# Eight idle matmuls placed at four products, in the PSUM bank each product is about to write

## The chip, the core and the metric

The kernel runs on one core of one Trainium2 chip. The metric is the device time of one execution in microseconds (us). Its five engines are named as in the profile: PE is TensorE (matrix products; PEld is its weight load), DVE is VectorE, ACT is ScalarE, POOL is GpSimd and SP is SyncE, which here only issues transfers (DMAs). PE writes to PSUM, which has eight banks; DVE and ACT read it from there.

## The reference

Two blocks are computed one after the other, in float32, for 4 batches, 4 heads of 32, 1088 tokens and a model width of 128:

```python
def phi(x):                                    # r = 8
    a = np.einsum('rd,bhsd->bhsr', S1, x)
    b = np.einsum('rd,bhsd->bhsr', S2, x)
    return np.einsum('bhsi,bhsj->bhsij', a, b).reshape(*x.shape[:-1], r * r)
q_p, k_p = (phi(q), phi(k))
kv = np.einsum('bhsf,bhsd->bhfd', k_p, v)
z = np.sum(k_p, axis=2)
num = np.einsum('bhsf,bhfd->bhsd', q_p, kv)
den = np.einsum('bhsf,bhf->bhs', q_p, z)[..., None] + 1e-06
x = num / den                                  # then (B, S, H*D)
...
theta = x @ w_theta
zr, zi = x * np.cos(theta), x * np.sin(theta)
y = np.einsum('ts,bsd->btd', w_tok_r, zr) + np.einsum('ts,bsd->btd', w_tok_i, zi)
u = x + y
out = u + np.maximum(u @ w_ch, 0.0)
```

The products with the two 1088x1088 token matrices are most of the arithmetic.

## The kernel before

Every piece of work is registered as an operation ("op") with a number in the order of registration: an engine, the buffers it writes and reads, and a function that issues its instructions. The order in which the ops are issued is not that of registration. It is written out in the string ORDER, a list of the 1015 numbers 0 to 1014, and the string PLACES gives each buffer its slot. A PSUM buffer's slot (class "ps", 0 to 7) is one of the eight banks. Each engine runs its own ops strictly in the order of ORDER. Between engines an op waits for what it reads, and a buffer that takes over a slot waits until every reader of the buffer that had the slot is done: the pool of PSUM tiles has one tile per slot.

A filler is one matmul that computes nothing that is used: `spin` multiplies a zeroed 128x384 bfloat16 tile `idle` with 128 of its own columns. It writes to the PSUM buffer `nowhere`, which sits in bank 3. Ten of them form op 1, at the start. One more is op 126, a normal op of the order; it is the last use of `nowhere`, and behind it bank 3 goes to another buffer. The string SPINS adds fillers ahead of chosen ops, as pairs "op:count"; `Layout.issue` issues them just before the op's own instructions, on PE.

Batches 0 and 1 go first. For each batch a chain of tiny operations turns the Gram matrix of the keys into the key sums' small matrices. It has three products on PE, with DVE and ACT work between them. For batch 1 (function `chain`, with stage name "chain1") these are:

| op | what it is | writes to bank | waits for | the bank's buffer before, and its last reader |
|---|---|---|---|---|
| 166 | first product (`first`) | `tp`, 5 | op 164 (DVE, e1) and op 165 (ACT, e0) | Gram matrix `kk`, read last by op 164 |
| 172 | second product (`second`) | `np`, 4 | op 170 (DVE) and op 171 (ACT), both `tac` | key features of batch 3, read by op 228 (ACT) |
| 174 | sum over partitions with `ones` | `pt`, 1 | op 173 (DVE, m4) | key features of batch 1 (`kf`), read last by op 143 (DVE) |

Around them the order of PE is: op 126 (filler), 189 and 197 (transposes and features of keys), 166, 191, 227, 209, 203 (key features, and a small sum), 132 and 138 (products of key features and values, batch 1), 172, 439 and 441 (transposes of the query features of batch 0), 174, 144 (the last third of the products begun by 132 and 138), 443 (numerator of batch 0). The order of DVE there is: 163, 433, 164, 318, 434, 167 (reads `tp`), 435, 168, 436, 169, 437, 170, 438 (query features), 143 (outer products of batch 1's key features, read from PSUM bank 1), 173 (reads `np`), 452, 175 (reads `pt`). ACT copies the key features with ops 228, 204, 192 in this order, and later the transposed query features with 442 and 440.

Op 422 is the first of three products that form the levels of batch 0's queries (`levels`, function `lev`). It reads the small matrices `mv` and `mf` of batch 0, which the last DVE steps of batch 0's chain (ops 117 to 122) write.

Batches 2 and 3 share their token products in a Winograd form, and the last of these products is issued in pieces. Op 1010 is the very last transpose on PE (`turn` in `finish_turned`, one matmul instruction with the identity for 128 columns; `times` beside it multiplies the same columns by `w_ch`). It writes to bank 7 (`ut`), waits for op 999 (DVE, which adds the last piece of the product to `xT`), and follows op 1005 (transpose) and op 1006 (product with `w_ch`) of the piece before. The buffer that had bank 7 before was last read by op 979 (DVE).

## Time and profile before

| | |
|---|---|
| three runs | 222.03, 223.25 and 223.28 us (median 223.25) |
| the profiled execution | 221.87 us in all; its span, first to last instruction, 220.1 us |
| PE | busy 211.9 us, 96% of the span, 2045 matmul instructions |
| DVE | busy 173.8 us, 79% |
| ACT | busy 116.8 us, 53% |
| fillers in the trace (line 350) | 20: ten at 1.34 us, two at 4.92, four at 7.80, one each at 15.81, 19.29, 25.26 and 32.59 |

All times in views are in us from the start of the span. In the timeline a row merges neighbouring instructions of a kind: start, length from the first start to the last end, engine, line, what is written and read, and how many instructions. A matmul's row lasts longer than its share of the pipeline, since matmuls overlap: what counts for throughput is the distance from one start to the next. An arithmetic product of float32 operands is two matmul instructions. Most helpers share a line: L312 is any product through `mm`, L292 any DVE `tensor_tensor`, L694 and L1010 are transposes of keys and of query features, L710 is the ACT copy of key features, L1014 that of query features.

### The profile page before, as it was taken

How to read it: one execution, taken by the hardware profiler on the slowest of the kernel's cores; microseconds unless marked ns; L12 is line 12 of the kernel's file. 1: busy time of each engine (PE TensorE's matmuls, PEld its weight loads, DVE VectorE, ACT ScalarE, POOL GpSimd, SP SyncE). 2: the span in 40 equal slices, each digit the busy share in tenths (PEclk: the TensorE clock that was granted, in tenths of full speed). 3: DMA queues.
4: the chain of work that ended last, by engine and by line, in shares of the span. 5: the costliest groups of instructions: out<-in, count | busy, mean ns of one | idle time of the engine just before them, and what ended most of it. 6: DMA issues, size and time to landing. Idle time of an engine off the chain costs nothing.

```text
span 220.1 us, 5075 instructions
## 1 busy us (share of the span) xinstructions
PE 211.9 (96%) x2045; PEld 160.0 (73%) x2045; DVE 173.8 (79%) x395; ACT 116.8 (53%) x228; POOL 22.7 (10%) x44
## 2 busy tenths in 40 slices
PE   7999996999999999999999999999999999999993
PEld 3787895776678576766667668777688888788872
DVE  4799999999989998988906852899268899955651
ACT  3899989779978986646424455623484000000000
POOL 2465000000050110000222040000200000000000
PEclk9999999999999999999999999999999999999999
DMA  5999189993969763785345342003400002102453
GB/s 177 421 416 390 35 368 356 337 414 102 357 207 255 211 251 133 283 324 206 79 139 91 119 107 42 1 13 56 66 0 0 3 0 47 25 0 43 66 91 75
DMA packets 23195, 34.68 MB, mean 158 GB/s; under 512 B 17028, under 2 KB 18308, under 8 KB 20996
## 3 DMA queue, kind: packets, MB, share of 16 engines
q1 hardware_dynamic: 17908, 29.28, 37.8%
q0 software_dynamic: 1728, 4.65, 9.9%
q10 hardware_dynamic: 3536, 0.43, 1.3%
q8 instruction: 16, 0.26, 0.5%
q14 instruction: 7, 0.06, 0.1%
HBM read 27.48 MB, written 2.23 MB: 135 GB/s over the span
## 4 chain that ended last, share of the span: by engine, by line
PE 83%; DVE 11%; ACT 2%; issue 2%; POOL 1%; POOLq 0%
PE ps L312 74%; PE ps L1010 3%; DVE big L292 3%; DVE g L292 2%; PE ps L1043 2%; PE ps L350 2%; DVE lv L292 1%; PE ps L918 1%; DVE sm L299 1%; DVE hf L296 1%; DVE sm L292 1%; PE ps L694 1%; ACT big L605 1%; ACT g L697 1%; DVE big L296 0%
## 5 line engine op out<-in xcount | busy, mean ns | idle before, releaser
L312 PE MATMUL ps<-big,zs 128*128 128x384 f32 (+4 forms) x398 | 111.6, 423 | 0.4 <-DVE big L292 0.4
L312 PEld LDWEIGHTS ps<-big,zs 128*128 128x128 f32 x398 | 71.2, 190 | 26.7 <-issue 0.8
L1142 ACT COPY g<-ps 128x128 f32<-128x128 f32 (+1 forms) x3 | 0.9, 301 | 48.1 <-PE ps L1134 44.6
L557 ACT ACTIVATE big<-zs 128x1088 int32<-128x1088 uint32 (+1 forms) x18 | 21.1, 1178 | 6.4 <-DMA zs<-w_tok 4.7
L292 DVE CUSTOM_DVE_ANT_0 big<-big,big 128x2176 uint16<-128x2176 uint16 x17 | 21.7, 1284 | 1.5 <-ACT big L557 1.5
L312 PE MATMUL ps<-big,big 128*64 128x64 f32 (+2 forms) x208 | 21.6, 276 | 0.0
L555 ACT ACTIVATE big<-zs 128x1088 f32<-128x1088 f32 x17 | 20.6, 1216 | 0.2 <-DMA zs<-w_tok 0.2
L312 PEld LDWEIGHTS ps<-big,big 128*64 128x64 f32 (+1 forms) x208 | 16.7, 154 | 3.0 <-issue 0.5
L292 DVE TENSOR_TENSOR big<-big,big 128x544 f32<-128x544 f32 x24 | 16.7, 714 | 0.1
L1014 ACT COPY g<-ps 128x384 f32<-128x384 f32 x24 | 10.3, 485 | 11.1 <-PE ps L1010 10.1
L292 DVE TENSOR_TENSOR zs<-ps,g 128x768 f32<-128x768 f32 (+2 forms) x20 | 12.5, 629 | 3.0 <-ACT g L1056 2.6
L306 POOL DMA_DIRECT2D big<-hf x6 | 5.9, 985 | 82.6 <-DVE sm L296 40.7
L296 DVE TENSOR_SCALAR big<-big 128x1088 int32<-128x1088 int32 x17 | 12.1, 718 | 0.1
L292 DVE TENSOR_TENSOR g<-lv 128x768 f32<-128x768 f32 x12 | 11.0, 953 | 0.6 <-PE ps L312 0.5
L312 PEld LDWEIGHTS ps<-w,big 128*128 128x128 f32 x80 | 10.3, 192 | 1.6 <-issue 0.6
L299 DVE SCALAR_TENSOR_TENSOR g<-g,ps 128x384 f32<-128x384 f32 x12 | 6.5, 549 | 5.9 <-ACT g L1052 5.7
L312 PE MATMUL ps<-w,big 128*128 128x128 f32 x80 | 11.1, 277 | 0.0
L1052 ACT ACTIVATE g<-ps 128x384 f32<-128x384 f32 x12 | 5.7, 490 | 7.9 <-PE ps L312 5.3
L1010 PEld LDWEIGHTS ps<-ident,g 128*128 128x128 f32 x72 | 8.2, 141 | 2.3 <-issue 0.8
L1010 PE MATMUL ps<-ident,g 128*128 128x128 f32 x72 | 9.5, 275 | 0.0
L299 DVE SCALAR_TENSOR_TENSOR big<-ps,even,big 128x256 f32<-128x256 f32 (+1 forms) x10 | 4.8, 495 | 5.7 <-PE ps L312 5.7
L312 PE MATMUL ps<-g,sm 128*64 128x384 f32 x48 | 9.1, 499 | 0.0
(185 smaller groups left out, 335.6 us busy)
## 6 DMA issues: line engine op xcount, KB each, us to landing
zs<-w_tok SPq DMA_DIRECT2D x17, 1088.0 KB, 7.0
big<-k_l SPq DMA_DIRECT2D x6, 576.0 KB, 5.9
big<-hf POOLq DMA_DIRECT2D x6, 576.0 KB, 5.6
big<-q_l SPq DMA_DIRECT2D x4, 576.0 KB, 8.7
big<-v_l SPq DMA_DIRECT2D x4, 576.0 KB, 11.0
g<-big POOLq DMA_DIRECT2D x4, 192.0 KB, 3.7
out<-g SPq DMA_DIRECT2D x16, 48.0 KB, 1.8
g<-big POOLq DMA_DIRECT2D x2, 160.0 KB, 3.2
```

The lines of the kernel that those rows point to most:

```text
L292: eng.tensor_tensor(out=o, in0=a, in1=b, op=f)
L296: (eng or V).tensor_scalar(out=o, in0=a, scalar1=s1, scalar2=s2, op0=op0, **kw)
L299: (eng or V).scalar_tensor_tensor(out=o, in0=a, scalar=s, in1=b, op0=op0, op1=op1)
L306: op("G", 0.9, lambda: G.dma_start(dst(), src(), accum_op=ALU.add), w, r, fly=fly)
L312: T.matmul(o, lhs, rhs, start=start, stop=stop, skip_group_check=True)
L350: T.matmul(nowhere(), idle()[:, 0:P], idle(), start=True, stop=True, skip_group_check=True)
L555: op("A", 0.22 + n * 0.0009, lambda: A.activation(dfn(), words_of(raw(), n)[1].bitcast(F32), AF.Prelu, scale=2.0**-112, alpha=-(2.0**32)), ...
L557: op("A", 0.22 + n * 0.0009, lambda: A.activation(stp(), words_of(raw(), n)[0].bitcast(U32), AF.Copy, scale=2.0**-29), [stp], [raw])
L1010: T.transpose(tr()[:, i * P:(i + 1) * P], qp()[:, i * H + 2 * n:i * H + 2 * n + 2].rearrange("p h i j -> p (h i j)"), ident())
L1014: op("A", act(GW), lambda n=n, tr=tr, qT=qT: A.copy(qT()[:, n], tr()), [(qT, n)], [tr])
L1043: T.transpose(x()[:, i], xs()[:, off + i * P:off + (i + 1) * P], ident())
L1052: op("A", act(GW), lambda cs=cs, th=th: A.activation(cs()[:, 0], th(), AF.Copy, bias=ROUND), [(cs, 0)], [th])
```

## The change

Four pieces of SPINS are new (166:1, 172:5, 174:1, 1010:1), and one is gone (422:1). `Layout.issue` now has two phases. Up to and with op 126 (`L.parted`) a filler goes to `nowhere`, as before. Behind it, an op's buffers get their tiles first, and its fillers then write to the PSUM tile that the op itself takes over (`home`). ORDER and PLACES are the same.

```diff
 SPINS = (
-    "76:2 139:4 158:1 109:1 422:1 "
+    "76:2 139:4 158:1 109:1 166:1 172:5 174:1 1010:1 "
 )
...
         spins = dict(tuple(map(int, x.split(":"))) for x in SPINS.split())
+        shared = True
         for o in self.order:
-            for _ in range(spins.get(o.i, 0)):
-                fill()
+            n, home = spins.get(o.i, 0), None
+            if shared:
+                for _ in range(n):
+                    fill()
             for b in o.bufs:
                 if b.ap is None:
-                    b.ap = view(pools[b.cls](b.slot), b.shape, b.dt)
+                    raw = pools[b.cls](b.slot)
+                    home = raw if b.cls == "ps" else home
+                    b.ap = view(raw, b.shape, b.dt)
+            if not shared:
+                for _ in range(n):
+                    fill(home)
             o.fn()
+            shared = shared and o is not self.parted
...
-    def spin():
-        T.matmul(nowhere(), idle()[:, 0:P], idle(), start=True, stop=True, skip_group_check=True)
+    def spin(home=None):
+        T.matmul(nowhere() if home is None else view(home, (GW,), F32), idle()[:, 0:P], idle(), start=True, stop=True, skip_group_check=True)
...
         if not bs[0]:
-            op("P", 0.1, spin, [nowhere], [kvb[WARM]] if WARM < B else [idle])
+            L.parted = op("P", 0.1, spin, [nowhere], [kvb[WARM]] if WARM < B else [idle])
```

## The prediction

> **What bounds the kernel now.** I read the page first (PE busy 96% of the span), then the chain of waits, to see where that share is the limit and where it is not. From 22.61 us on it is a chain of DVE work, with 0.02 us here and there and two longer gaps; at 40.22 it passes to PE. Columns: start, length, what ran.

> ```profile
> 22.61 0.86 DVE g L292
> ...
> 38.25 1.81 DVE g L292 x2
> 40.06 0.11 DVE sm L804
> 40.17 0.04 issue
> 40.22 0.86 PE ps L312 x26
> 41.08 0.87 PE ps L312 x4
> ...
> 215.62 0.02 issue
> 215.65 0.30 DVE big L292
> 215.94 0.04 issue
> 215.99 0.34 PE ps L1134
> ```

> So the new fillers at ops 166, 172 and 174 lie where DVE is the limit, and PE work there costs only what reaches DVE or pushes PE's start at 40.22. From 40.22 to 214.3 PE is the limit, and only the last 2 us alternate between PE and DVE again.

> Third, PE's timeline around batch 1's chain. Brackets give PE's idle time before a row and who ended it.

> ```profile
> 32.59 0.33 PE L350 MATMUL ps<-idle 128*128 128x384 bf16 x1
> ...
> 33.17 0.57 PE L312 MATMUL ps<-sbk,g 128*64 128x64 f32 x12
> 34.40 0.47 PE L312 MATMUL ps<-sbt,sm 64*64 64x64 f32 x8 [0.66 <-ACT big L710]
> 34.80 0.92 PE L312 MATMUL ps<-sbk,g 128*64 128x64 f32 x24
> ...
> 36.46 0.88 PE L312 MATMUL ps<-g,big 128*32 128x64 f32 x48
> 38.39 0.83 PE L312 MATMUL ps<-sm,pbd 128*128 128x64 f32 x6 [1.05 <-DVE sm L292]
> 39.26 0.87 PE L1010 MATMUL ps<-ident,g 128*128 128x128 f32 x6
> 40.22 0.39 PE L312 MATMUL ps<-sm,ones 128*128 128x4 f32 x2
> 40.53 0.54 PE L312 MATMUL ps<-g,big 128*32 128x64 f32 x24
> ```

> 34.40 is op 166, 38.39 op 172, 39.26 ops 439 and 441, 40.22 op 174. There are two pauses, 0.66 and 1.05 us, and hardly one before op 174. (The 0.66 is put down to an ACT copy; the DVE row for op 164, 34.04 to 34.26, and ACT's for op 165, 33.78 to 34.13, say that op 164 came last.) PE's pace is the same before and after the pauses: twelve transposes take 1.53 us at 21.27 and 1.53 at 41.88.

> **What one filler costs.** Four at 7.80 take 0.81 us with 0.326 for a single one: (0.81-0.33)/3 = 0.16 us apart. The ten at 1.34 take 3.38 with 0.527 for one: (3.38-0.53)/9 = 0.32 apart. The second is PE at half pace at the start; from 7.8 us on every filler row is 0.33 long. I take 0.16 and keep 0.32 as the bound.

> **Removed, 422:1.** The filler at 25.26 is gone. Op 422 starts at 25.53, 0.11 us after the filler's 0.16 were over, so the filler did not hold it. Its first 18 matmuls take 0.70 us (to 26.23) where 18 of the same take 0.38 at 26.75: 14 of them start from 25.94 on, since the last DVE step that writes its matrices ends at 25.70+0.19 = 25.89. Gain 0; the cover is the DVE chain. Bounds 0 to -0.1.

> **Added, 166:1.** Its bank 5 holds the Gram matrix, which op 164 reads until 34.26. Op 166 needs that same op's result. So this filler cannot run in the pause; it starts with the pause's end and puts op 166 back by 0.16. Behind it on PE all that follows up to op 138 is late by 0.16. Who waits: op 167 on DVE starts at 35.80 behind DVE's own queue, while `tp` is ready at 34.87 (slack 0.93); ACT's copies of key features start at 36.81, and the products they read are issued by 36.53 (slack 0.28). Cost on the path 0; bounds 0 to 0.16.

> [...]

> **Added, 172:5.** Bank 4 was last read by op 228, the first of three ACT copies at 36.81, which ends at 37.14. The last product ahead of the pause starts at 37.34-0.22 (the length of one) = 37.12, at 37.28 with op 166's 0.16. So the fillers run from about 37.3 to 37.3+5x0.16 = 38.1. Op 172 starts at 38.39. They fit with 0.29 us to spare: cost 0. At 0.32 each, op 166's too, they end at 37.46+1.59 = 39.05, 0.66 late; that is the bound, used below. Queued behind are op 172, then 439 and 441, whose query features DVE ends at 38.24+0.96 = 39.20.

> **Added, 174:1.** Bank 1 holds batch 1's key features, which op 143 reads on DVE from 39.12 to 40.07. The filler can start at about 40.13 (PE took 0.06 from op 173's end at 40.16 to 40.22), so op 174 starts at about 40.29, 0.07 late; at most 0.16. Behind it op 144 is late by as much, but op 443 at 41.08 waits for ACT's copy of the query features after 0.17 us without a weight load. On the other side op 175 on DVE is held at 40.95 by op 452 (40.08 plus 0.95), with the sum ready at 40.61. I take 0, bounds 0 to 0.16.

> **Added, 1010:1.** Op 1006's two matmuls start at 215.55; at 0.11 apart (twelve in 1.50 at 212.79) they are through at 215.77, the filler at 215.93, op 1010 starts at 215.99. Bank 7 was left by op 979 at 212.07. This one is on the path with 0.06 us of room: I take 0.05, bounds -0.05 (the transpose at 215.99 lasts 0.33 where the one behind running work, at 215.44, lasts 0.27) to +0.16.

> No DMA, no DVE, ACT, POOL or SP instruction is moved, added or taken away.

> **Sum.** 0+0+0+0+0.05 = +0.05 us on the profiled execution's 221.87 (1.77 of them outside the span). That execution lies 1.38 below the median of the three runs, and all four (221.87, 222.03, 223.25, 223.28) form two levels 1.2 to 1.4 apart, far more than the sum. What parts them no view of one execution shows, so I cannot say on which level a median will fall: I forecast no change from their mean, 222.61+0.05 = 222.7.

> **Rivals.**
> - *A clock effect (faster).* PE works at half pace for some microseconds at the start, shown by the fillers' 0.53 against 0.33. If in the higher executions it fell back once after the chain, PE at 0.16/0.32 of its pace would need about 1.3/(0.32/0.16-1) = 1.3 us of work done in 2.6, which is the size of the gap between the levels. The stretch 37.34 to 40.22 is PE's emptiest, with 13 matmuls and 1.70 of 2.88 us busy; five full-width fillers bring it to about 2.5. Then the upper level goes and the time is 222.0. Against: here the pace after 40 us is full, and the longest pause is 1.05. The page's clock row stands at 9 also in the first slice, where fillers take 0.53, so it cannot decide. [...] Chance 0.22.
> - *The pause is too short (slower).* If in other executions PE is at half pace in the pause at 37.2, the five fillers end at 39.05, op 172 is 0.66 late, ops 439 and 441 with it, ACT's copies, op 443 and all of PE's 170 us behind. It decides once a filler costs over (38.39-37.3)/5 = 0.22 us. Op 439 has 0.87 us from op 172's start to its own; at half pace I let that grow by half, an estimate, to 1.3. Price +0.7 to +1.1: 223.4 to 223.8. For it: half pace exists. Against: no row after 7.8 us shows it. Chance 0.10.
> - *It does not do what it says.* The fillers of 166 and 174 run behind the pause's reader rather than in it. That I expect, at no cost; if the slack named is wrong, both are paid, 0.16+0.16: 223.0. Chance 0.10.

> **How the numbers follow.** The forecast has 0.58 at 222.7, and its own spread is the two levels, 221.9 to 223.3. The lower end 221.7 is the lower level less 0.2 (the gains bounded above, 0.1 and 0.05); the upper end 223.7 takes in most of the slow rival and both fillers on the upper level. About 1% is what a measurement of this kernel can tell from no change, 2.2 us: more than any term. Faster by that needs the clock rival and a comparison from the upper level with more than one fall saved: 0.07. Slower by that needs half pace and the upper level: 0.05. Within: 0.88.

> **What would show it.** In the changed trace, five fillers between 37.2 and 38.3, 0.16 apart, and op 172 within 0.1 of 38.39; op 166 at about 34.56, its filler starting only after the DVE row ending at 34.26; op 174 at 40.22 to 40.38; op 443 still at 41.08, held by ACT; op 1010 at 215.99 to 216.05. I am wrong if op 443 moves, if fillers are 0.53 long, or if PE's rows after 41 us have another pace than before.

## The result and the profile after

The changed kernel is faster by half a per cent: median 221.62 us against 222.34 in 15 executions each, ratio 0.9953 with the 95% interval 0.9930 to 0.9975 (0.6 to 1.6 us). The forecast of no change fell, and the time lies just below its range, whose lower end is 221.7. The executions say more than the medians: those of before run from 221.41 to 223.61, with six between 223.25 and 223.61 and none between 222.54 and 223.25; those of after run from 221.03 to 222.16. The upper level is gone.

The two profiled executions show none of this: 221.87 before, 222.07 after. First the timeline of PE after the change, at the rows shown before (start, length, engine, line, output and inputs, idle time before it):

```profile
34.88 0.34 PE L359 MATMUL ps<-idle 128*128 128x384 bf16 x1 [0.57 <-DVE sm L301]
35.15 0.42 PE L321 MATMUL ps<-sbt,sm 64*64 64x64 f32 x8
35.50 0.92 PE L321 MATMUL ps<-sbk,g 128*64 128x64 f32 x24
...
37.16 0.88 PE L321 MATMUL ps<-g,big 128*32 128x64 f32 x48
37.97 0.99 PE L359 MATMUL ps<-idle 128*128 128x384 bf16 x5
38.96 0.83 PE L321 MATMUL ps<-sm,pbd 128*128 128x64 f32 x6
39.82 0.87 PE L1019 MATMUL ps<-ident,g 128*128 128x128 f32 x6
40.69 0.32 PE L359 MATMUL ps<-idle 128*128 128x384 bf16 x1
40.85 0.33 PE L321 MATMUL ps<-sm,ones 128*128 128x4 f32 x2
```

All of it lies 0.57 us later than before, and that comes from the start: PE was at half pace for longer in this execution. The record of the granted clock in the trace begins with full clock at 7.19 us, before at 6.07; 1.12 us more at half pace lose 0.56. It shows in the nine key transposes, with no edit near them, here first of before and then of after:

```profile
5.56 1.40 PE L694 MATMUL ps<-ident,big 128*128 128x128 f32 x9
5.54 1.96 PE L703 MATMUL ps<-ident,big 128*128 128x128 f32 x9
```

Four points of the timelines split the rest:

| from, to | before | after |
|---|---|---|
| start of the span to op 172 | 38.39 | 38.96 |
| op 172 to op 443 | 38.39 to 41.08: 2.69 | 38.96 to 41.65: 2.69 |
| op 443 to the first 384-wide token product | 41.08 to 50.26: 9.18 | 41.65 to 50.45: 8.80 |
| that to PE's last row | 50.26 to 216.15: 165.89 | 50.45 to 216.35: 165.90 |

The fillers cost nothing between op 172 and op 443, and the filler at the end nothing either. But 0.38 us went away between 41 and 50 us, where nothing was edited. The row concerned is the last of three groups of twelve small float32 matmuls (the levels of batch 1's queries; two matmul instructions are one product). Before, with the half-precision products ahead of it and the row behind:

```profile
47.78 0.55 PE L312 MATMUL ps<-mv,hf 128*64 128x96 f16 x18
48.17 1.06 PE L312 MATMUL ps<-mf,big 128*64 128x96 f32 x12
49.16 0.94 PE L312 MATMUL ps<-w,big 128*128 128x128 f32 x6
```

and after:

```profile
48.35 0.55 PE L321 MATMUL ps<-mv,hf 128*64 128x96 f16 x18
48.74 0.68 PE L321 MATMUL ps<-mf,big 128*64 128x96 f32 x12
49.35 0.94 PE L321 MATMUL ps<-w,big 128*128 128x128 f32 x6
```

The same twelve matmuls, 1.06 us and 0.68. The chain of waits of before has the gap as "issue" at 48.84: no engine was waited for. I call it the stop.

So there were two theories. *Clock theory:* the upper level consists of executions in which PE falls to half clock once, after its emptiest stretch, and the fillers prevent it. *Position theory:* the added instructions shift where in PE's instruction stream its code is fetched, and the stop goes away in every execution.

### The profile page after: what moved, and what is told of

It is laid out like the page before. It is cut to its first block, busy times and chain, and to the rows that moved or that the text cites. A ratio compares the mean times of both kernels' runs of the same rounds, so it can differ in the third digit from the quotient of the medians.

```text
span 220.3 us, 5088 instructions
## 1 busy us (share of the span) xinstructions
PE 213.3 (97%) x2052; PEld 160.9 (73%) x2052; DVE 173.8 (79%) x395; ACT 117.0 (53%) x228; POOL 22.6 (10%) x44
## 3 DMA queue, kind: packets, MB, share of 16 engines
HBM read 27.48 MB, written 2.23 MB: 135 GB/s over the span
## 4 chain that ended last, share of the span: by engine, by line
PE 85%; DVE 8%; ACT 2%; issue 2%; DMA 1%; POOL 1%; POOLq 0%
PE ps L321 75%; PE ps L1019 4%; PE ps L359 3%; DVE big L301 2%; PE ps L1052 2%; DVE g L301 1%; PE ps L927 1%; DMA out<-g 1%; DVE lv L301 1%; PE ps L703 1%; DVE hf L305 1%; DVE sm L308 1%; ACT big L614 1%; ACT g L706 1%; DVE big L305 0%
## 5 line engine op out<-in xcount | busy, mean ns | idle before, releaser
L359 PE MATMUL ps<-idle 128*128 128x384 bf16 x27 | 8.0, 414 | 1.9 <-POOL idle L361 1.3
```

The source lines that it names most:

```text
L359: T.matmul(nowhere() if home is None else view(home, (GW,), F32), idle()[:, 0:P], idle(), start=True, stop=True, skip_group_check=True)
```

## The experiments

Each execution's mean granted clock is recorded, so falls can be counted: with the 3.4 us at half clock that e4's trace shows (41.2 to 44.6, below), the mean over 220 us is 1-0.5x3.4/220 = 0.992. Each kernel ran 12 times (e9 13 times) beside 29 to 35 executions of before on the same chip, three chips in all. The spellings in the diffs are relative to the kernel before unless said otherwise; fillers at op 172 always go to its own bank, by the changed `issue`.

**The kernel before again** (e1), no edit.

> The kernel before, unchanged, to see each execution's span beside its granted clock. Clock theory: executions above 223.2 us show a lower mean granted clock than the others (one stretch of some 3.4 us at half clock in 220 us would be 0.992), those below 222.6 show 0.996 to 1.000. Position theory (PE's small stop at 48.6 us comes from where its code is fetched): all executions have the stop, the twelve matmuls at 48.17 take about 1.06 us; it says nothing of the two levels, and the clock need not differ between them.

Six of 12 lie at 0.991 or 0.992, among them all four above 223.1; the other six, 0.999 or 1.000, lie at 221.31 to 222.10. Of the 99 executions of before that stood beside the experiments 50 lie at 0.990 to 0.992, and none above 223.0 is outside that: every execution on the upper level fell. The reverse does not hold. Of the 50, 37 are above 223.0, and 13, at 0.990 or 0.991, lie at 222.01 to 222.34 (two such in e1), so there are falls that cost less; no trace has one. The clock theory's first half is shown. The stop was there but smaller, 0.80 us for the twelve matmuls:

```profile
47.93 0.80 PE L312 MATMUL ps<-mf,big 128*64 128x96 f32 x12
```

**The five fillers alone** (e2).

```diff
-    "76:2 139:4 158:1 109:1 422:1 "
+    "76:2 139:4 158:1 109:1 422:1 172:5 "
```

> The kernel before with the five fillers of op 172 alone (422:1 kept). Clock theory: they are what fills the emptiest stretch, so no execution lies above 222.9, and the median is about 222.0. Position theory: ten more PE instructions ahead of 48 us, where the whole change has twelve, so the stop at 48.6 is gone too and the lower level comes down by about 0.38, to 221.0 to 222.2. With both, ratio about 0.995 to 0.996.

Median 221.48, ratio 0.9946 (0.9918 to 0.9973), none of 12 fell, highest 221.97; the twelve matmuls take 0.68. The five fillers at op 172 alone have the whole gain of the change.

**The change without them** (e3): 166:1, 174:1 and 1010:1 stay, 422:1 is removed.

```diff
-    "76:2 139:4 158:1 109:1 422:1 "
+    "76:2 139:4 158:1 109:1 166:1 174:1 1010:1 "
```

> The changed kernel without the five fillers of op 172 (166:1, 174:1, 1010:1, and 422:1 removed, stay). Clock theory: the upper level returns, some 4 in 10 executions 1.2 to 1.4 us above the others with a granted clock near 0.992. Position theory: only two more PE instructions than before ahead of 48 us, so the stop of 0.3 to 0.4 us at 48.6 may be back; if it is, the lower level is that of before (221.4 to 222.5). Ratio 1.00.

Ratio 1.0006 (0.9968 to 1.0043); four of 12 fell, at 223.40 to 223.54. One more, at 223.89 with 0.997, stays unexplained. The stop is there, 1.05 us.

**Five narrow fillers** (e4): the changed kernel, those of op 172 with 8 columns.

```diff
+NARROW = (172,)
...
-                    fill(home)
+                    fill(home, 8 if o.i in NARROW else 384)
...
```

> The changed kernel, its five fillers at op 172 8 columns wide instead of 384: as many PE instructions, hardly any work for the array. Clock theory: the upper level returns in some 4 of 10 executions. Position theory: the stop at 48.6 stays away as in the changed kernel, and the lower level stays at 221.0 to 222.2. If the times are the changed kernel's in both respects, the number of instructions is all that matters.

Six of 12 fell, up to 223.52; those at full clock have a median of 221.37. The twelve matmuls take 0.68. So e4 parts the two theories: the number of instructions removes the stop, the width of the fillers holds the clock. The profile caught a fall. Busy time by engine in four consecutive stretches; PEclk is the granted clock:

```profile
34.40:37.80 3.40, 2.98 (x95) 2.62 (x95) 3.33 (x10) 3.40 (x9) 0.00 (x0) 1.00 1.01 428
37.80:41.20 3.40, 2.65 (x45) 2.11 (x38) 3.40 (x8) 2.18 (x6) 0.00 (x0) 1.00 0.80 281
41.20:44.60 3.40, 3.40 (x35) 2.05 (x28) 3.37 (x13) 2.00 (x4) 0.00 (x0) 0.50 1.01 406
44.60:48.00 3.40, 3.40 (x29) 2.32 (x28) 2.04 (x9) 2.82 (x7) 0.00 (x0) 1.00 1.00 413
```

The emptiest stretch, 37.8 to 41.2, is followed by one of the same length at 0.50, just where PE becomes the limit. Its cost in the timeline of the same kernel:

```profile
41.72 1.55 PE L322 MATMUL ps<-g,sm 128*64 128x384 f32 x4
43.20 2.20 PE L1020 MATMUL ps<-ident,g 128*128 128x128 f32 x12
45.24 0.83 PE L322 MATMUL ps<-w,big 128*128 128x128 f32 x6
```

The same rows of before:

```profile
41.08 0.87 PE L312 MATMUL ps<-g,sm 128*64 128x384 f32 x4
41.88 1.53 PE L1010 MATMUL ps<-ident,g 128*128 128x128 f32 x12
43.24 0.83 PE L312 MATMUL ps<-w,big 128*128 128x128 f32 x6
```

0.87 and 1.53 us before, 1.55 and 2.20 here; the row at 45.24 is at full pace again. From op 443 to the first 384-wide product it takes 51.88-41.72 = 10.16 instead of 8.80, which after takes without the stop: this fall costs 1.36 us. The profile of after happens to have an almost equal start (op 172 at 38.96, here 38.89), and with full-width fillers in the pause:

```profile
37.90:41.30 3.40, 3.36 (x45) 2.35 (x37) 3.40 (x8) 2.20 (x5) 0.00 (x0) 1.00 0.85 286
41.30:44.70 3.40, 3.40 (x49) 2.64 (x40) 3.37 (x13) 3.12 (x7) 0.00 (x0) 1.00 1.01 413
```

PE is busy 3.36 of 3.40 us, and the clock stays at 1.00.

**Two fillers** (e5, "422:1 172:2").

> The kernel before with two fillers at op 172 instead of five (422:1 kept). Clock theory: 0.32 us of full-width work instead of 0.81 in the same stretch; if any matmul there were enough, no execution falls to 0.992; if the amount counts, some of 12 still fall, fewer than the 18 in 35 of before. Position theory: four more PE instructions ahead of 48 us, between the two of e3 (stop of 0.37) and the ten of e4 (no stop), so the twelve matmuls take 0.68 to 1.05 us.

None of 12 fell; median 221.38, ratio 0.9943 (0.9920 to 0.9966); the stop is gone with four more instructions. Two do what five do.

**Ten fillers** (e6, "422:1 172:10").

> The kernel before with ten fillers at op 172 (422:1 kept): 1.6 us of them in a pause of 1.05. Clock theory: no execution at 0.992. The pause overflows by about 0.45 us: ops 172, 439 and 443 come 0.3 to 0.5 later than behind five fillers, and with no slack behind op 443 the median is 0.3 to 0.5 above that of five alone (221.48), about 221.9. If DVE's queue hides it, op 443 stays 2.69 us behind op 172's former place and the median is 221.5.

None of 12 fell; median 221.49. The overflow is real and costs nothing:

```profile
36.78 1.80 PE L359 MATMUL ps<-idle 128*128 128x384 bf16 x10
38.41 0.75 PE L321 MATMUL ps<-sm,pbd 128*128 128x64 f32 x6
39.00 0.85 PE L1019 MATMUL ps<-ident,g 128*128 128x128 f32 x6
39.69 0.38 PE L321 MATMUL ps<-sm,ones 128*128 128x4 f32 x2
40.00 0.54 PE L321 MATMUL ps<-g,big 128*32 128x64 f32 x24
40.80 0.87 PE L321 MATMUL ps<-g,sm 128*64 128x384 f32 x4 [0.26 <-ACT g L1023]
```

Against e5, whose full clock begins within 0.1 us of this one (4.70 and 4.77), with these rows,

```profile
38.11 0.83 PE L321 MATMUL ps<-sm,pbd 128*128 128x64 f32 x6 [0.46 <-DVE sm L301]
40.80 0.87 PE L321 MATMUL ps<-g,sm 128*64 128x384 f32 x4
```

op 172 is 0.30 later and op 443 in the same place. Ops 439 and 441 follow op 172 at once, and ACT's copies set op 443. My expectation of 0.3 to 0.5 us was wrong; the one that DVE and ACT hide it held.

**422:1 removed and 1010:1 added, no more** (e7).

> The kernel before with 422:1 removed and 1010:1 added, nothing at ops 166, 172, 174. Clock theory: the stretch around op 172 is as empty as before, half of the executions at 0.990 to 0.992, median as before; ratio 1.00. Position theory: two PE instructions fewer ahead of 48 us, the stop stays. The filler at the end costs 0 to 0.1 us: op 1010 starts 0.43 to 0.53 behind op 1006.

Three of 12 fell, fewer than half but not none; median 221.53, ratio 0.9976 (0.9947 to 1.0005). The profile is of a fallen execution (op 443 at 41.58, four matmuls in 1.55 us). Its end is that of before: op 1010 starts 0.43 behind op 1006, where before had 0.44 (215.55 to 215.99). In this trace the twelve matmuls take 0.68, at another time than usual because of the fall, so it says nothing of the stop at full clock.

**Ten more instructions where PE waits for DVE** (e8): five 8-column fillers to `nowhere` at op 422, none in the pause.

```diff
+THIN = {422: 5}
...
                 fill()
+            for _ in range(THIN.get(o.i, 0)):
+                fill(8)
...
```

> The kernel before with five more fillers, 8 columns wide, at op 422, where PE waits for DVE; nothing in the pause. Ten more PE instructions ahead of 48 us as with five fillers at op 172. Position theory: the stop is gone, the twelve matmuls take 0.68 us where before had 1.06, and the executions at full clock come out 0.1 to 0.4 us lower than those of before. Clock theory: half of the executions still at 0.990 to 0.992, up to 223.6, since the pause is as empty as before; median 221.9 to 222.3. A rival, that the number of PE instructions ahead of the pause also sets the clock, has no execution at 0.992.

The twelve matmuls take 0.68; four of 12 fell, up to 223.56. Those at full clock have a median of 221.26, those of before on that chip 221.79; for e4 it was 221.37 against 221.50. These are 6 to 17 executions each, and e7's nine at full clock, with fewer instructions instead of more, also have 221.37. So the position alone removes the stop, far from the pause, but what that is worth in the time rests on the traces, 0.12 (e1) to 0.38 us (before). In all profiles with the stop (before, e1, e3) the view of DMA queues has an instruction packet between 45.9 and 48.0 us and none between 43.5 and 45.8, of before:

```profile
q8 instruction: 1, 0.02, 2.9%
```

In after, e2 and e4, and in e5, e8, e10 and e11, it is the other way round: one between 43.5 and 45.8, none later; in e6 it starts at 43.08. The lead of that packet's start over the start of the row goes with the stop: 1.63 us in before (stop 0.38), 1.79 in e3 (0.37), 2.00 in e1 (0.12), and no stop at 2.47 (e7) and more. In e7 and e9 (3.73) the packet is a late one too, but the fall has put the row back. That PE stopped for lack of this packet's code is the likely reading; no run moves the packet alone.

**One filler** (e9, "422:1 172:1").

> The kernel before with one filler at op 172 (422:1 kept), 0.16 us of full-width work in the pause. Clock theory with a threshold on the amount of work: between none (half of the executions fall) and two (none of 12 did), so some of 12 fall, 1 to 5. If one matmul that breaks the pause is enough, none. Position theory: two more PE instructions ahead of 48 us, as in e3, so the stop of 0.1 to 0.4 us in the twelve matmuls may stay.

One of 12 fell (223.59). A thirteenth execution, the profiled one, was disturbed at the start (PE at half pace up to some 14 us, 226.84 in all) and is left out; it has a fall of its own, from 44.73 us. Ratio 0.9983 (0.9957 to 1.0009). On this chip 9 of 29 executions of before fell, so 1 of 12 is hardly a difference: that one filler helps is not shown.

**Five transposes in place of five fillers** (e10).

```diff
-    "76:2 139:4 158:1 109:1 422:1 "
+    "76:2 139:4 158:1 109:1 422:1 172:5 "
...
+        if turn:
+            T.transpose(view(home, (P,), F32), ident(), ident())
+            return
```

> The kernel before with five transposes of a 128x128 float32 tile at op 172 in place of five fillers (422:1 kept), 0.12 us each, 0.6 in all. If any busy PE counts for the clock, 0.6 us is more than the 0.32 of two fillers, and no execution falls to 0.992. If transposes do not count as busy for the clock in the same way, some 4 to 7 of 12 fall, up to 223.5, as with nothing in the pause. Position theory: five more PE instructions, or ten with their weight loads, so the stop is gone.

None of 12 fell, against 9 of 29 of before on this chip; median 221.44, ratio 0.9968 (0.9947 to 0.9990). Float32 transposes seem to hold the clock too, five of them in a row of 0.77 us in this profile (37.33 to 38.10); twelve executions make that likely, not certain.

**The changed kernel again** (e11).

> The changed kernel again, beside the same runs of before. Clock theory: none of 12 at 0.990 to 0.992, highest below 222.3, median 221.3 to 221.7. If the 15 executions were luck, some of these fall.

None of 12 fell; median 221.44, highest 222.12, ratio 0.9971 (0.9949 to 0.9992). With the first 15, none of 27 fell.

| fillers at op 172 | fell, of executions |
|---|---|
| none: before beside e1 to e4, e5 to e8, e9 to e11 | 18 of 35, 23 of 35, 9 of 29 (50 of 99) |
| none: e1, e3, e7, e8 | 6, 4, 3 and 4 of 12 |
| five of 8 columns (e4) | 6 of 12 |
| one (e9) | 1 of 12 |
| two, five, ten (e5, e2, e6) | 0 of 12 each |
| five, with the other edits (after, e11) | 0 of 27 |
| five transposes (e10) | 0 of 12 |

No version beat the change clearly. "422:1 172:2" does as well with less, 221.38 against 222.34 on its chip; it was not run beside the changed kernel.

## Why the prediction was wrong

- **The costs were right.** 0.16 us a filler (five in 0.99: (0.99-0.33)/4 = 0.17), 166's filler behind its bank's reader (34.88, the reader ended at 34.83), op 172 where it was but for the start, op 174 0.06 late (0.07 said), op 443 and op 1010 not late. The sum of the edits' own work is 0 (+0.05 said).
- **The failing step is the weighing of the clock rival**, 0.22, "Against: here the pace after 40 us is full, and the longest pause is 1.05". The sum has nothing for the fall. The profile was one execution that had not fallen, and about half of them do; its full pace says nothing of the others. The three times 222.03, 223.25 and 223.28 were the better evidence: two on the upper level. The mechanism, place and size of that rival (2.6 us at half pace, 1.3 us lost, upper level gone, 222.0) are what e1, e2 and e4 showed: 3.4 us and 1.36 us. "The page's clock row ... cannot decide" was wrong too: the row misses the start, but a fall in mid-run is in it, in e4 as a 7 among nines in the eighth slice. And the interval of 0.9930 to 0.9975 tells half a per cent from no change, where the prediction thought 1% was needed.
- **A term was missing from the sum**: the stop. "No DMA, no DVE, ACT, POOL or SP instruction is moved" overlooked the DMA queue that carries instructions (q8, 16 packets, 0.26 MB): with twelve more instructions ahead of the row its packet starts at 44.58 instead of 46.54, though PE is 0.57 later. The row of 1.06 us beside two of 0.68, and 0.06 us of "issue" between two PE pieces of the chain, could be seen in the profile of before.
- **The short-pause rival** (0.10) needs PE at half pace in the pause, and no trace has that; its step from a late op 172 to a late op 443 fails in e6, where DVE and ACT cover 0.30 us. The 0.66 us that it names was not tried. **"It does not do what it says"** was half right: the fillers of 166 and 174 run behind the pause and do nothing (e3), at no cost.
- Of the mean gain of 0.95 us (222.56 to 221.61 over 15 each), 222.56-221.98 = 0.57 is the upper level's six executions against the mean of the other nine. The other 0.38 has the size of the stop in two traces (before and e3), but the lower level of before also holds fallen executions (222.0 to 222.5 at 0.990 and 0.991 beside the experiments and in e4), so the two cannot be parted exactly.

## What to carry to other kernels

Where a few repeated times form levels, look for what differs between executions before pricing an edit on one of them: the granted clock of each execution told it at once. An edit that costs nothing on the path can still act through PE's clock, as the five fillers at op 172 did (0 of 12 fell in e2, 6 of 12 with narrow ones in e4), in the stretch behind the emptiest one, and that matters where PE becomes the limit right there (1.36 us for the fall in e4). A gap with no releaser in a row of equal instructions may be code fetch, an estimate from this one of 0.38 us: with ten more instructions ahead of it (e2, e8) it was gone, with two more (e3) it stayed, at 0.37.

## What was not expected of the hardware

PE fell to half clock with no long pause: the emptiest stretches before a fall had 2.65 (e4), 2.30 (e7) and 2.58 us (e9, 41.3 to 44.7) of 3.40 busy, and a longest pause of 0.71, 0.97 and 0.68 us. The prediction had counted a longest pause of 1.05 us against a fall.

```profile
37.30:40.70 3.40, 2.30 (x42) 1.82 (x30) 3.36 (x9) 2.19 (x6) 0.00 (x0) 1.00 0.78 274
40.70:44.10 3.40, 3.40 (x35) 2.03 (x35) 3.37 (x13) 2.24 (x5) 0.00 (x0) 0.50 0.99 395
36.80:40.20 3.40, 2.23 (x52) 1.75 (x40) 3.33 (x11) 2.21 (x7) 0.00 (x0) 1.00 0.81 258
```

The profiles of after and e11 also have a mean clock of 0.997 and 0.996, since the clock drops inside the span, at 218.82 and 218.47, behind PE's last matmul. If that mean marks a late start, it shows, by the same estimate, executions that would have fallen: it stands in 16 of the 75 executions with two or more full-width fillers or five transposes, in one of the 99 of before, and in e3's unexplained one. e6 has none, so its 0 of 12 says less than that of the others.

Busy time alone is not what decides: the stretch of before had 2.23 us busy and was not followed by a fall, that of e4 2.65 and was. What decides stays open.
